# Activation tiles loaded in pairs, the first one split by rows, in an attention + SwiGLU block

## The chip, the cores and the metric

The kernel runs on one core of a Trainium2 chip. The metric is the device time of one execution in microseconds. Six executions of the kernel before took 212.99 to 214.73 us, median 213.88.

## What is computed

The input x has 2048 tokens of 512 features in bf16. It is normalized per token (layernorm without scale), and two branches read the result: linear attention with 32 heads of 16, and a SwiGLU feed-forward of width 1792. The output is x plus both.

```python
xn = layernorm(x)
q, k, v = split_heads(xn @ wqkv)                 # 32 heads of 16
pq, pk = phi(q), phi(k)                          # phi(t) = where(t > 0, t + 1, exp(t)) + 1e-6
kv = einsum("bhsd,bhse->bhde", pk, v);  z = sum_s pk
o = einsum("bhqd,bhde->bhqe", pq, kv) / (einsum("bhqd,bhd->bhq", pq, z)[..., None] + 1e-6)
out = x + o @ wo + (silu(xn @ w_gate) * (xn @ w_up)) @ w_down
```

## The kernel before

The tokens are cut into 16 tiles of 128. A tile of x is 128 x 512 bf16, 128 KB, and lies in `x_sb[:, t, :]` with one token per partition.

The work has three parts. In the first, each tile gets its statistics on VectorE (step S, `bn_stats` and `bn_aggr`), is normalized (L on VectorE, P on GpSimd, A on ScalarE), transposed, and multiplied with the key and the query weights on TensorE (steps K and k for the keys, Q and q for the queries, all `proj`, L390). ScalarE, GpSimd and VectorE then form phi of the products (x, m, s for the keys; y, n, u for the queries), and TensorE accumulates the sum of xn times phi(k) over all tiles (step G, L439). In the second part TensorE computes gate and up products for 56 blocks (L521), and ScalarE and VectorE form silu(g) * u. In the third, woven into the second, each output tile takes 4 matmuls for the attention branch (L605) and 14 for the down projection (L609), x is added on VectorE, and the tile is stored.

The program is a list of operations that names for each what it reads and writes. `_Program` works out the waits from these names and emits the list engine by engine, so the order on an engine is the order in which the Python code adds its operations. A load is one entry with its own semaphore; an operation that reads its data waits for all of it. The order of the first part is written out by hand as a string of steps, a letter and a tile number each (L488 to L498). It begins:

```
S0 M1 a0 b0 c0 R0 d0 F2 C1 S3 e0 N0 W1 r0 K0 o0 f0 R3 w1 S2 K1 P3 k0 S1 R2 J0 W3 x0 k1 Q1 L2 R1 w3
m0 X2 q1 r1 Z2 Q3 s0 x1 o1 q3 S5 y1 K3 m1 k3 R5 n1 s1 G0 z1 L5 J1 x3 S9 K2 D5 Q0 z3 m3 S4 k2 R9 q0
```

Tiles 0 and 1 take a shortcut: they are only centred (a and b for the halves of tile 0, M and C for tile 1), and the scale is applied later. Tile 0 is transposed in two halves by TensorE (c0, d0; copied out by e0 on ScalarE and f0 on VectorE), tile 1 in one piece (W1, w1), tiles 3 and 2 likewise (W3 with w3, X2 with Z2); the other tiles go through DMA transposes issued by SP (D, L373). Eight matmuls on constants (`keep_busy`, L247) occupy TensorE while the first loads are under way, and F2 adds two more.

For tiles 0 to 3 a projection is cut in two by the contraction: K0 multiplies the first two of four blocks of 128 features with the first half of the key weights, k0 the other two with the second half. Q and q do the same with the query weights. Each half is one load of 256 KB, `wpart(eng, i, h)`, with i = 1 for keys and 0 for queries and h the half: a block of 128 rows by 512 columns, twice. The rest of `wqkv`, `wo` and the feed-forward weights come later from SP (L499 to L508).

The first loads are spread over the DMA queues of SP and ACT (ScalarE), L215 to L225. Tile 0 comes in two column halves (`xhalf`), one on each queue; then SP takes tiles 1 and 3, ACT takes tile 2, each of them two of the four weight halves, and SP tiles 4 to 15 one by one. On ACT these issues stand ahead of ScalarE's first work, behind a table load (L205). `xk(t)` (L253) gives the names that a reader of tile t waits for: two for tile 0, one for the others.

Of the kernel before, what the change touches and what calls it, by code (L numbers as in the profile page):

```python
# [9 lines left out]
P = 128  # L10
# [98 lines left out]
def bass_parallel_sum__linear_attn_block__swiglu_ffn__prompt_kernel(nc, A_x, A_wqkv, A_wo, B_x, B_w_gate, B_w_up, B_w_down, out):  # L109
    xin = A_x[0]  # L110
    oview = out[0]
    K = _Program()
    bf, f32 = dt.bfloat16, dt.float32

    with contextlib.ExitStack() as es:
        E = es.enter_context

        def sb(name, shape, dtype):
            return E(nc.sbuf_tensor(name, shape, dtype))

        x_sb = sb("x_sb", [P, NT, D], bf)
# [56 lines left out]
        def load(eng, key, dst, src):  # L178
            K.add(eng, lambda e: e.dma_start(dst, src), w=[key], dma=True)  # L179

        def xload(eng, t):
            load(eng, ("x", t), x_sb[:, t, :], xin[t * P:(t + 1) * P, :])
# [23 lines left out]
        H = D // 2  # L206

        def wpart(eng, i, h):
            load(eng, ("wqkv", i, h), wqkv[:, 2 * h:2 * h + 2, i * D:(i + 1) * D],
                 A_wqkv[2 * h * P:(2 * h + 2) * P, i * D:(i + 1) * D].rearrange("(c p) f -> p c f", p=P))  # L210

        def xhalf(eng, t, h):
            load(eng, ("x", t, h), x_sb[:, t, h * H:(h + 1) * H], xin[t * P:(t + 1) * P, h * H:(h + 1) * H])

        xhalf("sp", 0, 0)  # L215
        xhalf("act", 0, 1)
        xload("sp", 1)
        xload("act", 2)
        xload("sp", 3)
        wpart("act", 1, 0)  # L220
        wpart("sp", 1, 1)
        wpart("act", 0, 0)
        wpart("sp", 0, 1)
        for t in range(4, 16):
            xload("sp", t)  # L225

        K.add("pool", lambda e: e.memset(eps5[:, :], 1e-5), w=[("eps5",)])
        K.add("pool", lambda e: e.memset(ident[:, :], 0.0), w=[("ident",)])
# [478 lines left out]
```

## Time and profile before

| What | Value |
|---|---|
| median of six executions | 213.88 us (212.99 to 214.73) |
| the profiled execution, its own time | 214.73 us |
| its span in the profile | 213.5 us |
| TensorE busy | 209.8 us, 98% of the span |
| VectorE, ScalarE, GpSimd busy | 129.6, 70.1, 61.8 us |
| DMA, mean over the span | 75 GB/s, 15.91 MB |
| loads of x from SP, 128 KB each | 14 issues, median 4.9 us from issue to landing |
| halves of tile 0 (SP, ACT), 64 KB each | 2.0 and 2.2 us to landing |
| weight halves from ACT, 256 KB each | 2 issues, median 5.6 us to landing |
| weight halves from SP, 256 KB each | 2 issues, median 6.1 us to landing |

The span is the time between the first and the last record of the program on the core; the execution's own time has 1.23 us more around it. A share of busy time is an average over the whole span, so what a change in the first ten microseconds does has to be read there. "Landing" is when the last of the engines that carry a transfer has reported it. [...] successive matmuls overlap, and the distance between their starts is what counts.

### The profile page before, as it was taken

Reading aid. Unit: us, or ns where it says so; the run is one execution under the profiler, and the core shown is the slowest. Engines: PE = TensorE matmul, PEld = TensorE weight load, DVE = VectorE, ACT = ScalarE, POOL = GpSimd, SP = SyncE. Lnnn points to the kernel's source line nnn. Section 1 sums busy time; section 2 is a strip of 40 time slices with the busy share of each in tenths; the row PEclk is TensorE's granted clock in tenths of the full one; section 3 lists DMA queues with packets and bytes.
Section 4 is the critical chain, followed back from the end, with each engine's and each line's share of the span. In section 5 each row is a group of like instructions: output and inputs, shape, how many; then the busy total and the mean of one; then the engine's idle time right before and its main releaser. Section 6 shows DMA issues by size and latency. Waiting matters only on the chain.

```text
span 213.5 us, 2735 instructions
## 1 busy us (share of the span) xinstructions
PE 209.8 (98%) x1011; PEld 96.8 (45%) x1011; DVE 129.6 (61%) x227; ACT 70.1 (33%) x145; POOL 61.8 (29%) x90
## 2 busy tenths in 40 slices
PE   8899999999999999999999999999999999999996
PEld 3344444444544444444444444444444444444455
DVE  3689998992675697655646584654739462532122
ACT  4489888704364333021120322131223122130000
POOL 3478877799800522202202220210203000000000
PEclk9999999999999999999999999999999999999999
DMA  5923444299950011102011011101011101100101
GB/s 163 360 69 77 74 76 85 39 328 364 365 173 0 3 38 35 25 25 52 16 33 25 26 28 49 25 25 49 3 49 25 48 3 49 28 25 0 49 28 49
DMA packets 27453, 15.91 MB, mean 75 GB/s; under 512 B 17328, under 2 KB 27440, under 8 KB 27440
## 3 DMA queue, kind: packets, MB, share of 16 engines
q1 hardware_dynamic: 26608, 15.01, 25.5%
q10 hardware_dynamic: 832, 0.72, 1.0%
q8 instruction: 8, 0.13, 0.3%
q14 instruction: 5, 0.04, 0.1%
HBM read 9.70 MB, written 2.10 MB: 55 GB/s over the span
## 4 chain that ended last, share of the span: by engine, by line
PE 96%; DMA 2%; ACTq 0%; ACT 0%; DVE 0%; issue 0%
PE pb L521 45%; PE pb L609 23%; PE pb L390 14%; PE pb L605 6%; PE pb L439 6%; DMA wqkv<-in_A_wqkv_dram 2%; PE pb L546 0%; PE pb L599 0%; PE pb L357 0%; ACTq L179 0%; ACT L205 0%; DVE out_sb L615 0%; PE pb L562 0%
## 5 line engine op out<-in xcount | busy, mean ns | idle before, releaser
L529 ACT ACTIVATE sil<-pb 128x512 bf16<-128x512 f32 x56 | 33.3, 597 | 101.2 <-PE pb L521 98.8
L534 DVE TENSOR_TENSOR hT<-pb,sil 128x512 bf16<-128x512 f32 x56 | 38.0, 686 | 37.0 <-PE pb L521 34.1
L521 PE MATMUL pb<-xnT,wg 128*128 128x512 bf16 x224 | 57.8, 379 | 0.0
L521 PE MATMUL pb<-xnT,wu 128*128 128x512 bf16 x224 | 57.8, 379 | 0.0
L609 PE MATMUL pb<-wd,hT 128*128 128x512 bf16 (+2 forms) x252 | 51.4, 355 | 0.0
L571 POOL TENSOR_TENSOR pz<-pq,zbc 128x512 f32<-128x512 bf16 x16 | 18.6, 1163 | 89.5 <-DVE den L576 78.5
L609 PEld LDWEIGHTS pb<-wd,hT 128*128 128x128 bf16 x252 | 23.6, 98 | 24.9
L521 PEld LDWEIGHTS pb<-xnT,wu 128*128 128x128 bf16 x224 | 21.9, 98 | 25.9 <-DVE hT L534 0.2
L521 PEld LDWEIGHTS pb<-xnT,wg 128*128 128x128 bf16 x224 | 21.9, 98 | 25.8
L615 DVE TENSOR_TENSOR out_sb<-pb,x_sb 128x512 bf16<-128x512 f32 (+2 forms) x18 | 11.4, 632 | 33.3 <-PE pb L609 33.3
L390 PE MATMUL pb<-wqkv,xnT 128*128 128x512 bf16 x112 | 25.4, 379 | 0.0
L588 DVE TENSOR_TENSOR pq<-pq,rden 128x512 bf16<-128x512 bf16 x16 | 17.5, 1093 | 0.6
L418 POOL TENSOR_SCALAR ef<-ef 128x512 bf16<-128x512 bf16 x25 | 15.5, 622 | 5.8 <-ACT ef L411 5.5
L390 PEld LDWEIGHTS pb<-wqkv,xnT 128*128 128x128 bf16 x112 | 10.7, 98 | 13.7 <-DVE pk L429 0.7
L605 PE MATMUL pb<-M,pk 128*128 128x512 bf16 (+2 forms) x72 | 16.8, 355 | 0.0
L411 ACT ACTIVATE ef<-pb 128x512 bf16<-128x512 f32 x25 | 14.8, 593 | 3.8 <-PE pb L390 3.8
L257 DVE BATCH_NORM_STATS2 stats<-x_sb 128x6 f32<-128x512 bf16 x16 | 10.8, 677 | 3.0 <-DMA x_sb<-in_A_x_dram 3.0
L439 PE MATMUL pb<-pk,xn 128*128 128x512 bf16 x56 | 12.6, 379 | 0.0
L576 DVE TENSOR_REDUCE den<-pz 128x32 f32<-128x512 f32 x16 | 10.8, 674 | 0.0
L605 PEld LDWEIGHTS pb<-M,pk 128*128 128x128 bf16 x72 | 6.8, 98 | 7.4
L462 POOL TENSOR_TENSOR zacc<-zacc,pk 128x512 f32<-128x512 f32 x8 | 9.9, 1242 | 0.6
L429 DVE SCALAR_TENSOR_TENSOR pk<-pb,ef 128x512 bf16<-128x512 f32 x14 | 9.5, 682 | 0.6 <-POOL ef L418 0.3
(77 smaller groups left out, 113.5 us busy)
## 6 DMA issues: line engine op xcount, KB each, us to landing
out_dram<-out_sb SPq DMA_DIRECT2D x15, 128.0 KB, 1.7
x_sb<-in_A_x_dram SPq DMA_DIRECT2D x14, 128.0 KB, 4.9
wg<-in_B_w_gate_dram SPq DMA_DIRECT2D x2, 896.0 KB, 8.5
wu<-in_B_w_up_dram SPq DMA_DIRECT2D x2, 896.0 KB, 9.7
wd<-in_B_w_down_dram SPq DMA_DIRECT2D x2, 896.0 KB, 13.0
wqkv<-in_A_wqkv_dram ACTq DMA_DIRECT2D x2, 256.0 KB, 5.6
wqkv<-in_A_wqkv_dram SPq DMA_DIRECT2D x2, 256.0 KB, 6.1
wqkv<-in_A_wqkv_dram SPq DMA_DIRECT2D x1, 512.0 KB, 9.1
```

The costliest lines, as they stand in the source:

```text
L390: K.add("pe", [(lambda e, c=c: e.matmul(banks[b][:, :], src[:, c, t * P:(t + 1) * P], wqkv[:, c, col:col + D], start=(c == 0), stop=(c == ...
L411: K.add("act", lambda e: e.activation(buf, banks[b][:, :], ACT.Exp), r=[B(b)], w=[bkey])
L418: K.add("pool", lambda e: e.tensor_scalar(out=buf, in0=buf, scalar1=top, scalar2=0.0, op0=ALU.min, op1=ALU.max), r=[bkey] + tkeys, w=[bkey])
L439: K.add("pe", [(lambda e, c=c: e.matmul(banks[c][:, :], src[:, t, c * P:(c + 1) * P], pk[:, t, :], start=first, stop=last)) for c in range ...
L521: fns.append(lambda e, c=c, b=b, w_=w_: e.matmul(banks[b][:, :], w_[:, c, fc * P:(fc + 1) * P], xnT[:, c, C * 512:(C + 1) * 512], start=(c ...
L529: K.add("act", lambda e: e.activation(sil[:, j % 2, :], banks[gb(j)][:, :], ACT.Silu), r=[B(gb(j))], w=[("sil", j % 2)])
L534: K.add("dve", lambda e: e.tensor_tensor(out=hT[:, C % 2, fc, :], in0=banks[gb(j) + 1][:, :], in1=sil[:, j % 2, :], op=ALU.mult), r=[B(gb( ...
L571: K.add("pool", lambda e: e.tensor_tensor(out=pz[:, t % 2, :], in0=pq[:, t, :], in1=zbc[:, :], op=ALU.mult), r=[("pq", t), ("zbc",)], w=[( ...
L588: K.add("dve", lambda e: e.tensor_tensor(out=heads(pq[:, t, :]), in0=heads(pq[:, t, :]), in1=rden[:, i, :][:, :, None].broadcast_to([P, NH ...
L605: fns = [(lambda e, g=g: e.matmul(banks[bank][:, 0:hi - lo], pk[:, t, g * P:(g + 1) * P], M[:, g, lo:hi], start=(g == 0), stop=False)) for ...
L609: fns = [(lambda e, fc=fc: e.matmul(banks[bank][:, 0:hi - lo], hT[:, C % 2, fc, jj * P:(jj + 1) * P], wd[:, fc, lo:hi], start=False, stop= ...
L615: K.add("dve", lambda e: e.tensor_tensor(out=out_sb[:, t % 2, lo:hi], in0=banks[bank][:, 0:hi - lo], in1=x_sb[:, t, lo:hi], op=ALU.add), r ...
```

## The change

Tiles 2 to 15 are loaded two at a time: `xpair` is one DMA of 256 KB that writes `x_sb[:, t:t+2, :]`, two rows of 1 KB per partition. It stands for both tiles, so a reader of either waits for both. Tile 0 is still loaded by two DMAs of 64 KB, one per queue, but each brings 64 whole tokens (64 partitions, rows of 1 KB) instead of half of the features of 128 tokens (128 partitions, rows of 512 B). Its readers wait for both halves as before.

With that the lists of the two queues change. SP: half of tile 0, tile 1, second key half, second query half, six pairs. ACT: half of tile 0, the pair 2 and 3, first key half, first query half. Tile 3 has gone from SP to ACT. The number of loads issued for x goes from 17 to 10.

```diff
         def xhalf(eng, t, h):
-            load(eng, ("x", t, h), x_sb[:, t, h * H:(h + 1) * H], xin[t * P:(t + 1) * P, h * H:(h + 1) * H])
+            load(eng, ("x", t, h), x_sb[h * 64:h * 64 + 64, t, :], xin[t * P + h * 64:t * P + h * 64 + 64, :])
+
+        def xpair(eng, t):
+            K.add(eng, lambda e: e.dma_start(
+                x_sb[:, t:t + 2, :], xin[t * P:(t + 2) * P, :].rearrange("(a p) f -> p a f", p=P)),
+                w=[("x", t), ("x", t + 1)], dma=True)
 
         xhalf("sp", 0, 0)
         xhalf("act", 0, 1)
         xload("sp", 1)
-        xload("act", 2)
-        xload("sp", 3)
+        xpair("act", 2)
+        wpart("sp", 1, 1)
         wpart("act", 1, 0)
-        wpart("sp", 1, 1)
+        wpart("sp", 0, 1)
         wpart("act", 0, 0)
-        wpart("sp", 0, 1)
-        for t in range(4, 16):
-            xload("sp", t)
+        for t in range(4, 16, 2):
+            xpair("sp", t)
```

## The prediction, made before the changed kernel was run

> **What bounds the kernel now.** I read the page first: busy times, then the chain that ended last.
>
> ```profile
> PE 209.8 (98%) x1011; PEld 96.8 (45%) x1011; DVE 129.6 (61%) x227; ACT 70.1 (33%) x145; POOL 61.8 (29%) x90
> ...
> PE 96%; DMA 2%; ACTq 0%; ACT 0%; DVE 0%; issue 0%
> ```
>
> TensorE is busy for 98% of the span, and the chain is TensorE but for one DMA. So almost everything that the loads do is hidden, and only that one DMA's place can move the end. The chain in order of time, cut to the first 60 us, shows where it is:
>
> ```profile
> 0.80 0.43 ACT L205
> 1.23 0.04 issue
> 1.26 0.45 ACTq L179
> 1.71 0.03 issue
> 1.74 5.00 DMA wqkv<-in_A_wqkv_dram
> 6.75 0.14 issue
> 6.88 2.72 PE pb L390 x6
> ```
>
> The columns are start, length, what. ACT's queue issues x tile 2 at 1.26 (the line "ACTq L179"), then at 1.74 the first half of the key weights, `wpart("act", 1, 0)`, which I call wk0. It lands 5.00 us later, at 6.74; the first real matmul of the kernel, step K0 on L390, starts at 6.88. From there the chain is TensorE to the last drain: whatever shifts 6.88 shifts the end. The waits of TensorE in the first 50 us say the same: there are only two, and the first of them is the start of the program itself.
>
> ```profile
> PE pb L390 <- DMA wqkv<-in_A_wqkv_dram: 1.0, 1, 1.0
> PE pb L247 <- PEq L692: 0.8, 1, 0.8
> ```
>
> Is anything else nearly as late as wk0? The timeline before 7 us, for the other operand of K0 and the last work of TensorE before it:
>
> ```profile
> 3.02 0.69 DVE L257 BATCH_NORM_STATS2 stats<-x_sb 128x6 f32<-128x512 bf16 x1 [3.02 <-DMA x_sb<-in_A_x_dram]
> ...
> 5.08 0.69 DVE L257 BATCH_NORM_STATS2 stats<-x_sb 128x6 f32<-128x512 bf16 x1
> 5.11 0.37 ACT L365 ACTIVATE hT<-pb 128x256 bf16<-128x256 bf16 x1
> ...
> 5.22 0.61 PE L357 MATMUL pb<-ident,hT 128*128 128x128 bf16 x4
> ```
>
> Tile 0 starts its statistics at 3.02, when its two halves have landed, and its transposed copy is in SBUF at 5.11 + 0.37 = 5.48. TensorE finishes the transposes of tile 1 at 5.83. K0 could therefore start about 1.05 us sooner than 6.88 (6.88 - 5.83), and tile 0 has 6.74 - 5.48 = 1.26 us to spare against wk0.
>
> Last, the stages in one-microsecond stretches (columns: length, busy time of PE, PEld, DVE, ACT, POOL with counts, clock, DMA share, GB/s):
>
> ```profile
> 2.00:3.00 1.00, 1.00 (x4) 0.38 (x3) 0.00 (x0) 0.08 (x1) 0.62 (x3) 1.00 0.84 243
> 3.00:4.00 1.00, 1.00 (x4) 0.23 (x2) 0.91 (x3) 0.00 (x0) 0.00 (x0) 1.00 1.05 237
> 4.00:5.00 1.00, 1.00 (x7) 0.49 (x6) 0.64 (x3) 0.91 (x4) 0.00 (x0) 1.00 0.88 269
> 5.00:6.00 1.00, 0.83 (x6) 0.35 (x4) 0.96 (x4) 0.75 (x5) 0.53 (x3) 1.00 1.01 329
> 6.00:7.00 1.00, 0.12 (x1) 0.14 (x2) 1.00 (x3) 0.50 (x2) 0.53 (x3) 1.00 1.05 345
> 7.00:8.00 1.00, 1.00 (x3) 0.30 (x2) 0.93 (x4) 0.50 (x2) 0.89 (x3) 1.00 1.09 381
> ```
>
> The DMA engines are loaded throughout, at 237 to 269 GB/s up to 5.00 and 329 to 381 after. So wk0 lands late because other bytes go before it. Also, three matmuls in the microsecond from 7.00 mean about 0.43 us each; from about 10.2 the timeline has them at 0.216. The array is at half speed when K0 starts, although the clock column says 1.00.
>
> [...] the issues of the first microseconds land as tile 1 (SP), tile 2 (ACT), tile 3 (SP), wk0 (ACT), wk1 (SP), then the two query parts. [...]
>
> **The change part by part.**
>
> *Order of the rings (this decides).* Loads on each ring, in KB. Before: SP 64, 128 (tile 1), 128 (tile 3), 256 (wk1), 256 (query 1); ACT 64, 128 (tile 2), 256 (wk0), 256 (query 0). After: SP 64, 128, 256 (wk1), 256 (query 1), then pairs; ACT 64, 256 (tiles 2 and 3), 256 (wk0), 256. wk0 stays third on ACT, but tile 3 now stands before it on its own ring, and wk1 comes one place sooner on the other. What must move before wk0 is whole, if the rings take turns by whole transfers: before 64 + 64 + 128 + 128 + 128 + 256 = 768 KB, after 64 + 64 + 128 + 256 + 256 + 256 = 1024 KB. If they share byte by byte, both rings have moved as much as ACT's ring up to wk0: before 2 x 448 = 896, after 2 x 576 = 1152. Both ways it is 256 KB more. By the stretches above (28 kB before 2.00, from 14 GB/s over 2 us; then 271, 508, 777, 1106, 1451 kB by 3, 4, 5, 6, 7 us), 768 KB (786 kB) are through at 5.03 and 1024 KB (1049 kB) at 5.83: +0.80. Byte by byte: 917 kB at 5.43, 1180 kB at 6.21: +0.78. I take +0.8 for wk0: 6.74 to 7.54. An upper bound by place: wk0 lands where wk1 does now, 2.19 + 5.9 = 8.09 by the DMA answer, +1.35. Below: not before 5.69, when K0 would start at 5.83 as TensorE comes free, -1.05.
>
> *What a later K0 costs.* In a half-speed start as in this profile, all that follows is TensorE's own work: after 10.2 the starts of its matmuls leave two gaps beyond the pitch, 0.04 at 12.4 and 0.16 at 22.1, which a late start can absorb since the other engines then run ahead. So 0.8 - 0.1 = +0.7 on the profiled execution. In an execution where the array is already at full speed at K0, wk1 limits: four matmuls from 6.88 end at 7.75, step k0 waits for wk1 until 8.09 and ends at 8.09 + 0.43 = 8.52. After, wk1 has landed first, and six matmuls from 7.68 end at 8.98: +0.46. I take +0.6 between the two.
>
> *The issue of the pair.* No row has an x pair; the nearest, a 256 KB weight part of the same two-block shape, takes 0.456 on ACT against 0.449 for tile 2. wk0's issue moves by 0.01, between 0 and 0.05. Nothing.
>
> *Tiles 2 and 3.* Tile 3 needs the same bytes as before (512 KB by turns, 640 byte by byte), so it lands near its 1.73 + 3.1 = 4.83; tile 2 moves from 1.26 + 2.9 = 4.16 to that. Tile 3's statistics on DVE are queued at 5.08, before the two copies that free the second half of tile 0 and tile 1 at 6.49; TensorE wants these after 7.5. Cover 0.25 us for the first, over 1 us for the others. Tile 2's statistics start at 6.41: 1.6 us of cover. Cost 0; if the pair came at 5.5, DVE would slip by 0.4, still ahead of K1.
>
> *Tile 0 by rows.* 128 packets of 1 KB for 256 of 512 B, by the same two queues at the same times. Not in the trace. From below: 0.1 sooner, if packets of half the count save something of the 2.0 to 2.2 us to landing. From above: both halves go one after the other at half rate, 131 kB at 345 GB/s = 0.38 once more. Either is inside the 1.26 us to spare, so 0 on the path through tile 0; but lost DMA time would push wk0 by as much. I take 0 and keep +0.38.
>
> *Pairs from tile 4 on.* SP issues 6 for 12, which frees some 6 x 0.47 = 2.8 us of its 6.20 us row. The next on SP is a transpose at 14.65, which waits for data: nothing gained. Tile 5 is used at 12.27, over 2 us after it lands; the first of each pair comes about 0.4 later, inside that. The second query part, now ACT's last, lands perhaps 0.8 after its 2.23 + 6.1 = 8.33; step Q1 wants it near 11.2. Cost 0.
>
> Sum on the profiled execution: 214.73 us (span 213.5 and 1.23 around it) + 0.7 = 215.4. That execution is the slowest of the six; on the median of 213.88 I take +0.6, so 214.5.
>
> **The rivals.** Forecast, wk0 late by about 0.8: 214.5, chance 0.45.
>
> Rival 1, faster: the rings fill better. The place is 2 to 5 us, where 250 GB/s are moved against 345 and more later. With 256 KB transfers instead of 128 KB ones early in both rings, and 1 KB packets for tile 0, the rate might be the late one at once: 1049 kB at 381 GB/s from 2.00 are through at 4.68, 0.35 before the 5.03 of now; if in addition the last engine of wk0 trails less (landed 6.74 against 5.0 to 5.4 moved), K0 starts up to 1.05 sooner. It decides as soon as wk0 lands before 6.74. Price -0.35 to -1.05: about 213.1. For: the low early rate. Against: the DMA share of 0.84 to 1.05 says that the engines were loaded, with slow packets. Chance 0.2.
>
> Rival 2, no change: ACT's ring is served ahead of SP's, so wk1 does not come before wk0, and the 768 KB stay 768. For: the issues on the two queues are 0.01 apart. Against: SP was always one ahead. 213.9, chance 0.2.
>
> Rival 3, the clock: TensorE's idle stretch grows from 1.05 to 1.85 us, [...] Chance 0.15.
>
> **How the numbers follow.** The likeliest gives 214.5, its own range 214.1 to 215.2 (+0.25 to +1.35). About 0.5%, some 1.07 us, is what can be told from no change: the bounds are 212.8 and 214.95. Faster takes half of rival 1, 0.1. Slower takes rival 3, 0.15, and some 0.25 of the forecast (wk0 at wk1's place, or the 0.38 of tile 0 on top), 0.12: 0.27. The rest, 0.63, is within. The range from 212.9 to 215.7 leaves out rival 3 and the best of rival 1.
>
> **What would show it.** In the changed profile's chain, the DMA piece before L390 should be longer than 5.00, near 5.8, and L390 should start near 7.7; wk1 should land before wk0; no second wait of TensorE for a DMA should appear. Tile 0's statistics should start between 2.9 and 3.4. If L390 starts before 6.88, rival 1; at 6.9, rival 2; if matmuls at 0.43 us go on past 11, rival 3. I am wrong if TensorE is late for something other than weights.

## The result, and the profile after

The changed kernel takes 215.83 us (median of 17 executions, 213.43 to 217.69); the kernel before, run beside it, 213.66 (median of 38, 212.99 to 215.83). The ratio is 1.0081, 95% interval 1.0057 to 1.0104: it compares fast executions alone, without two slow ones of the changed kernel (217.47 and 217.69 us, mean clock 0.984), and isn't the ratio of the two medians, which is 1.010. By this ratio the change makes the kernel slower by 0.8%, some 1.7 us; by the medians it is 2.2 us.

The profiled execution of the changed kernel took 215.03 us, only 0.3 more than that of before. Its chain in order of time, the start (line numbers are four higher from here on: the projections are L394):

```profile
1.40 0.04 issue
1.44 4.53 DMA x_sb<-in_A_x_dram
5.97 0.02 issue
5.99 0.70 DVE stats L261
...
6.94 0.30 ACT lnv L268
7.24 0.11 issue
7.36 2.72 PE pb L394 x6
```

K0 starts at 7.36 instead of 6.88. The chain names ScalarE's logarithm for it, which no matmul reads. The first key half (wk0) lands at the same time: issued at 2.29, 4.9 us to landing, 7.22 in the trace, and K0 follows 0.14 later, as it did in the profile of before. So wk0 is taken to be the releaser, and the logarithm a coincidence. The DMA answer for that moment, the two key halves (SP's issued at 2.05, so landed near 6.45):

```profile
wqkv<-in_A_wqkv_dram SPq DMA_DIRECT2D x1, 256.0 KB, 4.4
wqkv<-in_A_wqkv_dram ACTq DMA_DIRECT2D x1, 256.0 KB, 4.9
```

wk0 takes 4.9 us to land, not the 5.8 of the forecast; it took 5.0 before. It is late because it is issued late: 2.29 instead of 1.74. The timeline of ACT's queue, the changed kernel first, then the one before (start, length of the issue):

```profile
0.84 0.56 ACTq L179 DMA_DIRECT2D x_sb<-in_A_x_dram  x1
...
1.44 0.82 ACTq L216 DMA_DIRECT2D x_sb<-in_A_x_dram  x1
...
2.29 1.01 ACTq L179 DMA_DIRECT2D wqkv<-in_A_wqkv_dram  x2
```

```profile
0.83 0.40 ACTq L179 DMA_DIRECT2D x_sb<-in_A_x_dram  x1
1.26 0.45 ACTq L179 DMA_DIRECT2D x_sb<-in_A_x_dram  x1
1.74 0.46 ACTq L179 DMA_DIRECT2D wqkv<-in_A_wqkv_dram  x1
```

The half of tile 0 takes 0.56 instead of 0.40 to issue, and the pair behind it 0.82, where the single tile 2 took 0.45. (The last line of the changed kernel holds two issues; wk0's own takes 0.49.) The second thing to see is the clock. The one-microsecond stretches of the changed kernel (PEclk is the third figure from the end):

```profile
5.00:6.00 1.00, 0.46 (x7) 0.29 (x4) 0.01 (x1) 0.52 (x4) 0.61 (x3) 1.00 1.09 378
6.00:7.00 1.00, 0.00 (x0) 0.00 (x0) 0.96 (x4) 0.06 (x1) 0.01 (x1) 1.00 1.09 367
7.00:8.00 1.00, 0.65 (x2) 0.29 (x3) 1.00 (x3) 0.43 (x2) 0.53 (x2) 0.51 1.08 364
8.00:9.00 1.00, 1.00 (x3) 0.30 (x2) 0.93 (x5) 0.50 (x2) 0.89 (x3) 0.50 1.12 359
9.00:10.00 1.00, 1.00 (x5) 0.44 (x4) 0.59 (x2) 0.00 (x0) 0.45 (x1) 0.50 1.11 349
10.00:11.00 1.00, 1.00 (x8) 0.64 (x7) 0.42 (x1) 0.89 (x2) 0.01 (x1) 0.78 1.09 346
```

Here the array was at full rate already: of its two matmuls of 256 columns at 4.86 the first is 0.27 long, both together 0.38, so their starts lie 0.11 apart. The trace's clock record has full rate from 3.60. Then TensorE has nothing to do from 5.46 to 7.36, 1.9 us, and from 7.02 to 10.43 the clock is at half rate (PEclk 0.51 and 0.50), then full again. A stretch like this, 3.4 us long here, is what the expectations below call a window. Half of the clock for 3.4 us is 1.7 in 213.7, 0.8% of the mean clock, so an execution that fell back once has a mean clock of 0.992. That gives a count without a profile: 12 of the 18 executions on record for the changed kernel lie below 1.00 (10 of 16 without the two left out), and 6 of 67 of the kernel before in the first set of runs below, 0 of 47 and 0 of 11 in the others. Those 6 have a median of 215.33 us, the other 61 one of 213.07. A mean of 1.00 doesn't rule out a slow start: in the first profile of before, the rate before its clock record begins at 10.1 is not in that mean, and only the distance of the matmuls (0.43) shows it. So the count may miss slow starts: of the six executions of the changed kernel at 1.00, three took 213.4 to 214.3 us and three 216.4 to 216.6.

### The profile page after: what moved, and what is told of

Its sections match the earlier page's. It is cut to its first block, busy times and chain, and to the rows that moved or that the text cites. A ratio compares the mean times of both kernels' runs of the same rounds, so it can differ in the third digit from the quotient of the medians.

```text
span 213.7 us, 2728 instructions
## 1 busy us (share of the span) xinstructions
PE 208.7 (98%) x1011; PEld 96.8 (45%) x1011; DVE 129.5 (61%) x227; ACT 70.3 (33%) x145; POOL 61.9 (29%) x90
## 4 chain that ended last, share of the span: by engine, by line
PE 96%; DMA 2%; DVE 1%; ACT 0%; issue 0%
PE pb L525 45%; PE pb L613 23%; PE pb L394 14%; PE pb L609 6%; PE pb L443 6%; DMA x_sb<-in_A_x_dram 2%; PE pb L550 0%; PE pb L603 0%; DVE stats L261 0%; PE pb L361 0%; ACT L205 0%; ACT lnv L268 0%; DVE out_sb L619 0%; PE pb L566 0%; DVE mv L264 0%
## 5 line engine op out<-in xcount | busy, mean ns | idle before, releaser
L394 PE MATMUL pb<-wqkv,xnT 128*128 128x512 bf16 x112 | 25.2, 379 | 0.0
L394 PEld LDWEIGHTS pb<-wqkv,xnT 128*128 128x128 bf16 x112 | 10.9, 98 | 13.3 <-DVE pk L433 0.4
```

Source lines behind the costliest of these rows:

```text
L394: K.add("pe", [(lambda e, c=c: e.matmul(banks[b][:, :], src[:, c, t * P:(t + 1) * P], wqkv[:, c, col:col + D], start=(c == 0), stop=(c == ...
```

## The experiments

The theory after this profile, A: TensorE's idle stretch ahead of the projections has grown, and in most executions the clock falls back to half rate for a stretch like that from 7.02 to 10.43. Its form A1 blames the late issue of wk0, A2 the late landing of tile 0. Rivals: B, the bytes ahead of wk0 (the forecast); C, issue time itself: the slow issues make TensorE wait longer, and the clock has no part in the loss.

**Rows alone and pairs alone.** Rows: the kernel before, with only this:

```diff
-            load(eng, ("x", t, h), x_sb[:, t, h * H:(h + 1) * H], xin[t * P:(t + 1) * P, h * H:(h + 1) * H])
+            load(eng, ("x", t, h), x_sb[h * 64:h * 64 + 64, t, :], xin[t * P + h * 64:t * P + h * 64 + 64, :])
```

> The kernel before with only tile 0 split by rows. Theory A (half-rate window): the loss of the change comes from TensorE's idle stretch ahead of K0 growing until a clock window falls back to half rate; rows alone lengthen the first issues on both queues from 0.40 to about 0.56, so the first key half lands about 0.2 later than 6.74, K0 at about 7.1, and some executions lose a window: +0.2 to +0.9 on the median, about 214.3. Theory B (bytes alone): no byte is moved ahead of the first key half, so 0 to +0.1. Theory C (issue time): the slow issue of 64-partition loads is the main cause, +1 or more.

Pairs: the changed kernel with that line as it was before.

> The changed kernel with tile 0 split by columns again. Theory A: the first key half still lands 0.4 to 0.8 later than before, the idle stretch is still about 1.7 to 2 us and the median loss is +1 to +1.7, most executions with a mean clock of 0.992. Theory B: +0.8, all of it wait for the key half, clock as before. Theory C: the issues on ACT are back to 0.40 and 0.45, and so is the time, within 0.3 of before.

Rows alone: ratio 1.0082 (1.0056 to 1.0109), 13 of 22 executions with a mean clock below 1.00. Pairs alone: 0.9999 (0.9970 to 1.0028), 1 of 14. The whole loss is in the rows, as theory C had it for the size and A for the clock; the size, about 2 us on the median, is beyond A's +0.2 to +0.9. B falls, and A's own expectation for the pairs with it. ACT's queue with rows alone, no pair in it:

```profile
0.84 0.58 ACTq L179 DMA_DIRECT2D x_sb<-in_A_x_dram  x1
1.45 0.83 ACTq L179 DMA_DIRECT2D x_sb<-in_A_x_dram  x1
2.31 0.46 ACTq L179 DMA_DIRECT2D wqkv<-in_A_wqkv_dram  x1
```

The 0.83 is tile 2 alone, 128 KB: so it isn't the pair that is slow to issue, it is whatever stands behind a half by rows. But this one profile shows the slow issues and not yet the loss:

```profile
6.91 2.72 PE L390 MATMUL pb<-wqkv,hT 128*128 128x512 bf16 x6 [0.89 <-DMA wqkv<-in_A_wqkv_dram]
```

It is a half-speed start, like the first profile of before (the six matmuls take 2.72 in both), and against that one wk0, issued 0.57 later, was 4.46 us on the way instead of 5.00, landed at 6.77 instead of 6.74, and K0 starts 0.03 later. It took 214.98 us, near that profile's 214.73. Whether a late issue of wk0 becomes a loss has to come from the runs that move it.

**Pairs only from tile 4 on**, everything else as before:

```diff
-        for t in range(4, 16):
-            xload("sp", t)
+        for t in range(4, 16, 2):
+            xpair("sp", t)
```

> Tiles 0 to 3 and the weight halves as in the kernel before, only tiles 4 to 15 in pairs. All theories: nothing that K0 waits for is moved, so within 0.2 of before, 213.7. If it is slower by more, late arrival of a pair or the load on the rings behind the weights matters, which nobody has put down.

0.9988 (0.9968 to 1.0008). The later pairs cost and gain nothing that can be measured.

**The idle stretch filled.** The changed kernel with more matmuls on constants, in the list of steps:

```diff
-S0 M1 a0 b0 c0 R0 d0 F2 C1 S3 e0 N0 W1 r0 K0
+S0 M1 a0 b0 c0 R0 d0 F2 C1 S3 e0 N0 W1 F10 r0 K0
```

> The changed kernel with ten more matmuls of 256 columns on constants between the transposes of tile 1 and K0, so that TensorE's idle stretch is filled by 1.1 us (at full rate) to 2.1 us (at half rate). Theory A: the window is kept at full rate, mean clock 1.00 in nearly all executions, and the median falls from 215.8 to 213.3 to 214.2. Theory B and C: the wait for the key half is the loss and filling it changes nothing, or costs up to 0.5 where the filler ends after the key half has landed: 215.8 to 216.3.

214.11 beside 213.09, ratio 1.0039 (1.0020 to 1.0057), and 22 of 22 executions at 1.00. Useless work on TensorE takes away about half of the loss, as A expected, and every fallback with it: that half is put down to the clock. How much exactly is less certain, since the intervals of 1.0039 and 1.0081 just touch. The timeline of TensorE:

```profile
5.98 1.28 PE L251 MATMUL pb<-const-bfloat16-1.0 128*128 128x256 bf16 x10
7.75 1.46 PE L394 MATMUL pb<-wqkv,hT 128*128 128x512 bf16 x6 [0.49 <-DMA wqkv<-in_A_wqkv_dram]
9.05 0.39 PE L361 MATMUL pb<-ident,xn 128*128 128x128 bf16 x4
```

wk0 lands at 7.62 and K0 starts at 7.75, after the filler has ended. The transposes behind the projections start at 9.05; in an execution of before near its median, shown further down, they start at 8.19. These 0.86 us are 0.4% of the span, one execution each, so the other half of the loss fits the late start.

**What of the rows does it?** Three runs separate the late issue of wk0 from the late tile 0. First, rows, with wk0 ahead of tile 2 on ACT (tile 0 still late); then the same order with columns; then columns with tile 2 in two column halves, so that wk0 is issued 0.49 later with the same bytes ahead (readers of tile 2 then wait for both halves, which the cut doesn't show):

```diff
+        wpart("act", 1, 0)
         xload("act", 2)
         xload("sp", 3)
-        wpart("act", 1, 0)
```

```diff
-        xload("act", 2)
+        xhalf("act", 2, 0)
+        xhalf("act", 2, 1)
```

> Tile 0 by rows, no pairs, and ACT issues the first key half directly behind its half of tile 0, ahead of tile 2; tile 0 itself stays about 0.25 late. Theory A1 (rows cost because the first key half is issued 0.56 later): that half is now issued at about 1.45 instead of 2.31 and lands near 5.5, so the loss of the rows alone (0.8%) is gone, 212.6 to 213.4, and mean clocks of 0.992 are as rare as in the kernel before (6 of 67). Theory A2 (rows cost because tile 0 and with it the transposes come 0.25 later): K0 and K1 still wait for what hangs on tile 0 and on VectorE, the half-rate windows stay in about half of the executions, 214.5 to 215.3.

> The kernel before with the first key half ahead of tile 2 on ACT, nothing else. Theory A1: K0 starts when TensorE comes free, the idle stretch shrinks, half-rate windows vanish and the median falls by 0.2 to 0.6 below before. Theory A2: no fewer half-rate windows than before; same as before within 0.2%. Tile 2 then lands near 5.4 and has to stay ahead of its statistics at 6.4; if it does not, up to 0.5 is lost again.

> Tile 0 by columns as before, but tile 2 on ACT in two column halves, so that the first key half is issued about 0.4 later (2.13 instead of 1.74) with the same bytes ahead of it. Theory A1: most of the loss of the rows appears without any rows: 214 to 215, mean clock 0.992 in a third or more of the executions. Theory A2: tile 0 is in time, so within 0.2% of before, 213.1 to 213.5.

Rows with wk0 first: 1.0023 (1.0008 to 1.0038), 2 of 22 below 1.00: most of the loss is gone although tile 0 is as late as with rows alone (its statistics start at 3.24 and 3.27), so A2 falls as the main cause; the median (213.66) is above what A1 expected.

Columns with wk0 first: 1.0008 (0.9987 to 1.0029), so the gain that A1 hoped for is not there. K0 does start at 5.43, as TensorE comes free, but k0 waits for wk1 until 7.84, and the transposes behind start at 8.29, no sooner than with wk0 in its old place.

Columns with wk0 late: 1.0115 (1.0080 to 1.0150), 5 of 6 below 1.00, with no row load in the kernel, and more than A1 expected. So a loss of this size needs no rows. It goes with a late wk0: issued 0.49 later, it lands at 8.22 in the profiled execution, with 5.99 us on the way. The issue alone doesn't explain a landing so late. Tile 2 also comes in twice as many packets of half the size here, and these may count: in the first 5 us as many packets move as in the second profile of before, shown further down (1022 and 1032), but fewer bytes (0.69 and 0.83 MB). The two aren't separated in this run; the run with tile 2 by rows below keeps the packets and loses no less.

**Tile 0 in one load on SP**, ACT starting with tile 2 (its readers wait for that one load):

```diff
-        xhalf("sp", 0, 0)
-        xhalf("act", 0, 1)
+        xload("sp", 0)
```

> Tile 0 in one load of 128 KB on SP; ACT starts with tile 2 and issues the first key half at about 1.26 instead of 1.74. Theory A1: the first key half lands 0.3 to 0.5 sooner, no half-rate windows, 212.5 to 213.1. Theory A2: tile 0 comes 0.1 to 0.3 later than by two column halves and the half-rate windows appear in a third or more of the executions: 213.6 to 214.8.

1.0075 (1.0050 to 1.0100), 9 of 18 below 1.00. A1's gain did not come: wk0 is in SBUF by 4.96, but in the profiled execution tile 0 is 0.5 late and tile 3 lands at 7.33. The statistics of tile 3 stand on VectorE ahead of the two copies that K1 and k0 need, so TensorE waits there instead, for a reason that neither A1 nor A2 had:

```profile
PE pb L389 <- DVE hT L366: 2.6, 1, 2.6
```

**The whole change with wk0 first**:

```diff
+        wpart("act", 1, 0)
         xpair("act", 2)
         wpart("sp", 1, 1)
-        wpart("act", 1, 0)
```

> The whole change, with one line moved: ACT issues the first key half ahead of the pair of tiles 2 and 3. Theory A1 (the late issue of the first key half, and with it a clock window at half rate, is the loss): the half is issued at about 1.45 instead of 2.30, mean clocks of 0.992 become rare (under one in five), and the median falls from 0.8% above before to 0.2 to 0.5% above, 213.6 to 214.2; what is left is tile 0 late by 0.25 and the pair landing behind the key half. Theory A2 (tile 0 late): 0.992 stays in half of the executions and the time within 0.2% of the changed kernel's.

1.0114 (1.0079 to 1.0149), 5 of 6 below 1.00. This missed, and A1 in its narrow form falls with it. K0's two matmuls start at 5.66, but the pair, now behind wk0 and behind the slow issue, lands at 7.05, and again VectorE holds the copies until tile 3's statistics are done. The timeline of TensorE:

```profile
5.66 0.59 PE L394 MATMUL pb<-wqkv,hT 128*128 128x512 bf16 x2
8.55 1.03 PE L394 MATMUL pb<-wqkv,hT 128*128 128x512 bf16 x2 [2.30 <-DVE hT L371]
```

So what counts is the last of two arrivals, wk0 and tile 3, and not wk0 alone. In the run with rows and wk0 first, tile 3 was a single load on SP, landed at 6.26, and TensorE's second wait, for the same copies, ended at 7.76.

**A second profile of before, and of pairs alone**, since the first ones of both were among their slower executions.

> The kernel before once more, for a second profile of it, since the first was among its slower executions. Theory A: an execution near the median of 213.1 has its full clock from about 3.5 to 6 us on and keeps it, K0 starts between 5.8 and 6.9 and the matmuls behind it are 0.216 apart. If it is at half rate up to 10 us like the first profile, theory A has the usual state of before wrong.

> The change with tile 0 by columns once more, for a profile near its median (the first look was its slowest execution). If the forecast's sum of bytes holds, the first key half lands about 0.8 later than in an execution of the kernel before of the same speed, hidden only because the second key half has then landed already; if it lands within 0.3 of it, the bytes did not count.

The timelines of TensorE, before (213.31 us), then pairs alone (213.10 us):

```profile
4.70 0.38 PE L247 MATMUL pb<-const-bfloat16-1.0 128*128 128x256 bf16 x2
5.03 0.40 PE L357 MATMUL pb<-ident,hT 128*128 128x128 bf16 x4
6.21 1.03 PE L390 MATMUL pb<-wqkv,hT 128*128 128x512 bf16 x4 [0.79 <-DMA wqkv<-in_A_wqkv_dram]
7.75 0.61 PE L390 MATMUL pb<-wqkv,hT 128*128 128x512 bf16 x2 [0.50 <-DMA wqkv<-in_A_wqkv_dram]
8.19 0.39 PE L357 MATMUL pb<-ident,xn 128*128 128x128 bf16 x4
```

```profile
5.25 0.45 PE L361 MATMUL pb<-ident,hT 128*128 128x128 bf16 x4
6.62 1.46 PE L394 MATMUL pb<-wqkv,hT 128*128 128x512 bf16 x6 [0.92 <-DMA wqkv<-in_A_wqkv_dram]
7.92 0.39 PE L361 MATMUL pb<-ident,xn 128*128 128x128 bf16 x4
```

In this execution of before, near its median, the array is at full rate early and stays so (the two matmuls at 4.70 take 0.38 together, PEclk is 1.00 from 3 to 12 us, and K0's four are done in 1.03); K0 starts at 6.21, and the idle time is cut in two by the four matmuls ahead of the wait for wk1, which lands at 7.71. With pairs alone wk0 lands 0.4 later (6.49 against 6.08), half of what the sum of bytes asked for, and all six matmuls follow at once, since wk1 is there at 6.28. The next transposes start at 7.92 against 8.19: pairs alone are not behind.

**Is a load of 64 rows slow to issue in another place too?** Columns for tile 0, tile 2 on ACT in two halves by rows:

```diff
-        xload("act", 2)
+        xrows("act", 2, 0)
+        xrows("act", 2, 1)
```

(`xrows` is `xhalf` as the change has it, 64 rows each.)

> Tile 0 by columns, tile 2 on ACT as two halves of 64 rows: the mirror of the run with tile 2 as two column halves (issues of 0.46 and 0.45 on ACT, first key half issued at 2.23). If a load of 64 partitions is slow to issue by itself, the two issues here take 0.56 to 0.85 each, the first key half is issued at 2.5 to 2.8, and the time is at least that of the column halves, 1.0 to 1.6% above before. If the slow issue belongs only to the first loads of the program, the issues are 0.45 and the time is that of the column halves, about 1.1% above.

1.0165 (1.0126 to 1.0205), 6 of 6 below 1.00. ACT's queue in it:

```profile
1.27 0.52 ACTq L179 DMA_DIRECT2D x_sb<-in_A_x_dram  x1
1.82 0.61 ACTq L179 DMA_DIRECT2D x_sb<-in_A_x_dram  x1
2.47 0.60 ACTq L179 DMA_DIRECT2D wqkv<-in_A_wqkv_dram  x1
```

The two halves take 0.52 and 0.61, where the column halves in the same places took 0.46 and 0.45, and wk0 itself takes 0.60 for 0.46. Smaller than at the start of the program, and wk0's issue at 2.47 is just short of the 2.5 expected, but the same sign: here too a load of 64 rows of 1 KB was slower to issue than one of 128 rows of 512 B, and so was what came behind it. At the start of the program the row length isn't it: with tile 0 in one load, 128 rows of 1 KB were issued in 0.40 on SP and 0.39 on ACT.

## Why the prediction was right and wrong

The forecast was 214.5, slightly slower; the ratio on its median of 213.88 gives 215.6, near the top of the range, and the measured median of 215.83 is just above it. The place was right, the reason mostly not, and that the forecast comes this near is luck: the term that it rested on cost nothing, and a term that it put at nothing cost it all. Of its signs, wk1 before wk0 came true (6.45 against 7.22); the load before K0, 4.9 us on the way instead of 5.8, did not.

*The bound.* Right: the first projections set the end. But that first profile was of a half-speed start; in the second profile TensorE waits twice, for wk0 and for wk1, and has no half-rate stretch after 5 us.

*Order of the rings, +0.8.* Mis-sized, and made up for. With pairs alone wk1 did land before wk0, but wk0 came only 0.4 later (6.08 to 6.49; in the first profiles, with other clocks, 6.74 to 6.78; one execution each), and wk1, 1.4 sooner, gave it back. What it costs at the end: nothing (0.9999). How the two queues share the DMA engines, by whole transfers or byte by byte, was assumed for the sums and shown by no run. The forecast's +0.46 for a full-speed start counted wk1's gain, but from a K0 that starts too late.

*Issue of the pair, nothing.* Right for the pair behind a column half: 0.46 with pairs alone. Behind a half by rows it took 0.82.

*Tile 0 by rows, 0 on the path.* This step failed: with rows alone it cost 0.8%, the whole loss. It priced the landing of tile 0, and had that right (statistics at 3.25 against 3.02, within its 1.26 to spare), but took "the same two queues at the same times" for granted. The halves take 0.16 longer to issue, and the next issue 0.15 longer on SP and 0.37 on ACT, so that wk0 left 0.55 late and wk1's queue 0.3 late. It priced the issue of the pair and not that of the halves ahead of it.

*Tiles 2 and 3.* With pairs alone the pair landed at 4.25 and 4.44, before the 4.83 of the forecast. In the changed kernel it landed at 5.97, beyond the 5.5 that the prediction looked at, and held VectorE from 4.94 to 5.99. There wk0 was still later; with wk0 first, and with tile 0 in one load, it was the late tile 3 that TensorE waited for.

*Pairs from tile 4 on.* Right, 0.9988.

*The rivals.* Rival 3, the clock, got 0.15. It is what happens in two of three executions, and by the run with the idle stretch filled it is about half of the loss. It had the growing idle stretch right (1.9 us, for the 1.85 that it named), with the wrong picture of the start: not a half rate that goes on past 11, but a full rate that had begun at 3.60 and fell back from 7.02 to 10.43. The profiles differ in when full rate begins: 3.6 in the changed kernel, 4.5 and 10.1 in the two of before. Rivals 1 and 2 did not come.

*Still open.* Why a load of 64 partitions is slower to issue, and why it slows the next one, no run shows. How long a wait can be without a fallback is known only roughly. In the profiles the full rate was lost where the longest wait of TensorE ahead of the projections was 1.7 us (the first profile of pairs alone), 1.9 (the changed kernel), 2.3 (the change with wk0 first) and 2.6 (tile 0 in one load, tile 2 in halves of either kind); it was kept at 0.8 (the second profile of before), 0.9 (pairs alone) and 1.1 (rows with wk0 first). That is one execution each; the counts over many executions are the firmer ground. The longest wait may not be the measure either. In the two profiles whose clock is followed here, the fall came 3.4 us after full rate had begun, with TensorE idle in one and at work in the other: from 3.60 to 7.02 in the changed kernel, where it was idle until 7.36, and from 6.09 to 9.51 with tile 2 in column halves, where it had been at work again since 8.36:

```profile
8.00:9.00 1.00, 0.64 (x3) 0.32 (x4) 0.37 (x1) 0.00 (x0) 0.23 (x1) 1.00 1.09 379
9.00:10.00 1.00, 1.00 (x7) 0.52 (x6) 0.00 (x0) 0.00 (x0) 0.00 (x0) 0.75 1.10 360
10.00:11.00 1.00, 1.00 (x6) 0.51 (x5) 0.42 (x1) 0.96 (x2) 0.10 (x1) 0.50 1.05 339
```

Of the last wait before the fall, 1.56 us lay inside the stretch at full rate in the changed kernel (5.46 to 7.02), 2.27 with tile 2 in column halves (6.09 to 8.36) and 1.49 with wk0 first (6.25 to the fall at 7.74; PEclk is 0.87 from 7 to 8). In the second profile of before two waits, 0.79 and 0.50, sum to 1.29, and the rate was kept. Whether the longest wait counts or the idle time inside that stretch, no run was made to test. No version tried is faster than the kernel before by more than its interval.

## What to carry to other kernels

When a DMA's shape is changed, look at the length of its issue and of the issue behind it on the same queue, not only at when it lands: here tile 0 had over a microsecond to spare and the load two places behind it had none. Where TensorE waits at the start, a longer wait can cost more than its own length, because the clock can fall back: here an issue 0.55 us later went with a loss of 1.7 us, about half of it the clock. The mean clock over many executions shows it, one profile may not. And take a second profile near the median before reasoning from the first.

## What the runs showed of the hardware

- A load of 64 partitions x 1 KB took 0.56 to 0.58 us to issue as the first on SP or ACT (five profiles), one of 128 partitions x 512 B took 0.39 to 0.41 (eight), one of 128 partitions x 1 KB 0.39 and 0.40 (one). The load behind it on ACT took 0.82 to 0.84, whether it had 128 or 256 KB, instead of 0.45 or 0.46 behind a load of 128 partitions (0.52 where it was itself one of 64).
- In six profiles, with a wait of 1.7 to 2.6 us ahead of the projections, TensorE's clock fell back to half rate; in the two followed here that was 3.4 us after full rate had begun (3.60 to 7.02 and 6.09 to 9.51). By the mean clock it stayed there for 3.4 us in five of them (0.992) and for 6.8 in one (0.984, the change with wk0 first). Ten matmuls on constants in the changed kernel's idle stretch took the share of executions with a fallback from 12 of 18 to 0 of 22.
- Full rate began at 3.6 us in the changed kernel's profile, at 4.5 and 10.1 in the two of the kernel before, whose TensorE had the same eight matmuls on constants up to 4 us.
